# Gated linear attention and a squared-ReLU layer: another opening, joined score stretches, and attention pairs at other places

## The chip, the cores and the metric

The kernel runs on one core of a Trainium2 chip. The time is device microseconds of that core; 523.65 us is the median of three runs of the kernel before (522.74 to 524.44). The engines are named as in the profile: PE (TensorE), DVE (VectorE), ACT (ScalarE), POOL (GpSimd), SP (SyncE, which issues all transfers here).

## What is computed

The inputs q, k, v and alpha have shape (4, 8, 768, 48) in float32. `moe_w_in` (384 x 2048) and `moe_w_out` (2048 x 384) are float64.

```python
for t in range(S):
    state = alpha[:, :, t, :, None] * state + np.einsum('bhd,bhe->bhde', k[:, :, t], v[:, :, t])
    y[:, :, t] = np.einsum('bhd,bhde->bhe', q[:, :, t], state)
...
x = np.ascontiguousarray(attn_out.transpose(0, 2, 1, 3)).reshape(B * S, H * D)
...
h = np.maximum(x @ w_in, 0.0)
return (h * h @ w_out).astype(np.float32)
```

## The kernel before, in words

**Attention blocks.** The 768 steps are cut into 6 chunks of 128, and with 4 batches this makes 24 blocks; block n is chunk n // 4 of batch n % 4. For one block: the logarithm of alpha (`ln`), its running sum by a matmul with a triangle of ones (`cs`), exp of it and of its negative (`eb`, `ei`), q and k scaled by them (`mq`, `mk`), both transposed (`qT`, `kT` in the first four blocks, `turn` for a pair later) and copied from PSUM to SBUF (`qc`, `kc`), products of k and q (`scores`) and of k and v (`state_sums`) in halves of 64 rows, the masked copy of the products (`masked`, called am), the sum with the old state (`sums_copied`, called us) and the next state (`next_state`, called st). The next state is multiplied by the block's last decay: `bl` writes one row of 1.5 KB to DRAM (SP, line 297), `br` reads it back turned into two columns of `last_t` (SP, line 303, two transfers), and DVE multiplies by it on line 421.

**Pairs.** Blocks are worked on in pairs. `ga(a, n)` does scores and state for block n and begins y of the pair a, a+1 that came before; `gb(a, n)` does block n+1 and ends y of the old pair. y is copied into x with `ev` (12 copies per pair, on ACT; for the pairs beginning at 0 and 2, 6 of them on DVE).

**Weights.** Each of the two matrices comes in 8 parts of 768 KB (`load_weights`). The float64 words are turned into float32 in three calls: `convert_first` (2 DVE instructions), `convert_middle` (2 ACT), `convert_second` (3 DVE, lines 175, 179 and 182). Four raw buffers hold parts before conversion. A part of w_in serves two h tiles of 128 columns.

**The dense layers.** The tokens go in 6 groups of 512 (4 blocks). Group 0 runs in plain float32: `ffn_in(0, j)` for 16 h tiles j (3 matmuls each, two records per matmul in the profile, line 805), then the second layer (`layer_out`, `out_plain`, `out_x`, `out_y`, line 701). From group 1 on the products are made in three passes of rounded parts (`in_x`, `in_y`, line 622; `out_x`, `out_y`). For these, x is split (`split_x`, `diff_x`: xa on ACT, xl and xd on DVE), h is split (`split_h`, `diff_h`), and the weights are split once (`prepare`: cast, rest, scale, diff) and kept in DRAM (`keep`), from where `pump` streams them.

**The order.** Nothing is scheduled automatically: each engine runs its instructions in the order in which the program emits them, and each waits for what it needs. The opening is a list of words (`first`), one call per word; it covers blocks 0 to 3, the conversion of the first weight parts, and h tiles 0 and 1, each in two halves of 256 tokens (`ha`, `hb`; the second half needs x of blocks 2 and 3). After that `weave` runs a list of dense units, each with a cost, and emits an event as soon as the costs run reach the event's time. Times for the events are in `AT` and in `PLAN`, in units of these costs: one unit is about 1.3 us. `attention` makes the events of pairs from `PLAN`; `g0`, `g1` and `g` are the places where pairs begin within group 0, group 1 and the later groups, `sc0` stretches them in group 0. Each group has its own call of `weave` with times from 0.

**Transfers.** All transfers are issued by SP in program order. Eight semaphores are used in turn, so a transfer also waits until the one eight places before it has landed.

Of the kernel before, what the change touches and what calls it, by code (L numbers as in the profile page):

```python
# [18 lines left out]
AT = {'evs': 0.4, 'lead': 4, 'post': 3, 'w_first': (46.0, 49.5, 53.0), 'wstep': 1.6, 'w_in_at': 2, 'w_in_by': 3.4, 'room1': 22, 'room': 25, 's0': 4, 'ahead': 6, 'late': 2, 'xs': 0.2, 'g0': (-0.5, 19.5, 28.0), 'sc0': (2.35, 2.35, 2.35), 'g1': (2.5, 19.5, 35.0), 'g': (2.2, 15.0), 'g1x': 50, 'gx': 46, 'g0x': 55.5, 'k0': 2, 'h0': 18, 'k1': 4, 'h1': 4, 'h1by': 2, 'evs0': 0.8, 'tp': 'ADMD', 'tp1': 'ADAD', 'split': 8, 'o0': (40, 47), 'o1': (), 'o2': (23, 26, 29, 35, 42, 36), 'str1': 24, 'ga': 10, 'gb': 12.5}  # L19
# [6 lines left out]
def kernel(  # L26
# [77 lines left out]

    def load(n, xs="aqkv"):
        c, b = divmod(n, B)
        for x in xs:
            t = tile_of(x, n)
            nc.sync.dma_start(  # L109
                out=t[:, :, 0:D] if x in "qk" else t.rearrange("a (h d) -> a h d", h=H),  # L110
                in_=srcs[x][b, :, c * C : (c + 1) * C, :].rearrange("h s d -> s h d"),
            )
# [49 lines left out]
    def convert_middle(i):  # L162
        if moe_w_in.dtype == FP32:
            return
        w, lo, hi, power, upper = half[i]
        nc.scalar.activation(
            out=power, in_=power, func=AF.Relu, scale=2.0**23, bias=rebias
        )
        nc.scalar.activation(out=w, in_=lo, func=AF.Copy, scale=2.0**-52, bias=1.0)

    def convert_second(i):
        if moe_w_in.dtype == FP32:
            return
        w, lo, hi, power, upper = half.pop(i)
# [67 lines left out]
    def ln(n):  # L242
        la = blk[n]["la"] = tile_of("a", n)
        nc.scalar.activation(out=la, in_=la, func=AF.Ln)
# [15 lines left out]
    def cs(n):  # L260

# [26 lines left out]
    def mq(n):  # L288
        scaled("q", n, blk[n]["b"])

    def mk(n):
        scaled("k", n, blk[n].pop("inv"))

    def bl(n):

        if n // B < NCH - 1:
            nc.sync.dma_start(out=rows_t[n], in_=blk[n]["b"][C - 1 : C, :])

    def br(n):
        if n // B < NCH - 1:  # L300
            row = rows_t[n].rearrange("a (p e d) -> (a d) e p", e=2, d=D)
            for e in range(2):
                nc.sync.dma_start(out=last_t[n % 4][64 * e : 64 * e + D, :], in_=row[:, e])  # L303

    def turned(x, n):
        rows = tile_of(x, n).rearrange("a h d -> a (h d)")
# [70 lines left out]
    def masked(n):  # L377
        ps = two[n]
# [10 lines left out]
    def state_sums(n):  # L389
        ps = two[n]  # L390
# [11 lines left out]
    def sums_copied(n):  # L402

        ps = two.pop(n)
# [9 lines left out]
    def next_state(n):  # L414
        blk[n]["s"] = s_t[n % B]
        if n // B < NCH - 1:
            s_all.append(s_t[n % B])
# [12 lines left out]
    def inner(product, m, p, e, h):  # L430
        head = 2 * p + e
        return product(
# [40 lines left out]

    def turn(n):

        for m in (n, n + 1):
            ps = blk[m]["T"] = [bank(m, "T", (2, NP, 64)) for _ in range(2)]
# [14 lines left out]
    def ev_part(n, p):  # L492
        ev(n, (p,))
# [4 lines left out]
    def ev(n, ps=tuple(range(NP))):  # L498
        g, t = divmod(n, GB)
        if t == 0 and ps[0] == 0:  # L500
# [48 lines left out]
    def cast_w(w, p):  # L549
        b = here["b", w, p] = wt("wb", FP32R, shapes[w])  # L550
# [58 lines left out]
    def split_x(g, kk):  # L609
        if kk == 0:  # L610
# [30 lines left out]
    def in_y(j):  # L641
        in_passes(j, "d", "d", False, True)
# [5 lines left out]
    def in_post(j):  # L648
        if kinds[0][j % 4] == "D":
# [31 lines left out]
    def split_h(n, i):  # L681
        r = i % (AHEAD + MORE)
# [34 lines left out]
    def out_plain(p, t, pieces):  # L717
        if p == 0:
# [81 lines left out]
    def ffn_in(g, j, cols=slice(0, GB * C)):  # L800
        w, c0 = w_in[j * NW // NJ], j % (NJ // NW) * 128
        n = cols.stop - cols.start
        ps = ps_ffn.tile([128, GB * C], FP32, tag="att", name="h")[:, 0:n]
        for kk in range(KM):
# [3 lines left out]
            )  # L808
        r = two_k("r")[:, 0:n]
# [10 lines left out]
    def ffn_out(g, t, i):  # L820
# [27 lines left out]
    steps["ha"] = lambda j: ffn_in(0, j, slice(0, HT))  # L848
    steps["hb"] = lambda j: ffn_in(0, j, slice(HT, 2 * HT))
    steps["first"], steps["middle"], steps["second"] = convert_first, convert_middle, convert_second  # L850
    first = """
        ln0 cs0 ei0 mk0 warm0 eb0 bl0 mq0 kT0 load0v kc0 ln1 qT0 load2a load2k cs1
        eb1 qc0 mq1 sc0 bl1 kv0 qT1 load1v ei1 mk1 load2q load3a kT1 ln2 qc1 load3k
        cs2 br0 am0 kc1 eb2 sc1 weights0 br1 us0 kv1 zeros2 bl2 load2v am1 ei2 us1
        load3q ya0 ln3 cs3 yb0 eb3 weights1 mk2 ei3 load3v mq2 qT2 st0 ev0 kT2
        zeros2 zeros2 zeros2 kc2 first0 mk3 middle0 kT3 mq3 br2 load4v qc2 kc3 bl3
        weights2 qT3 sc2 load4q qc3 kv2 second0 am2 br3 first1 sc3 weights3 us2
        load4a kv3 am3 us3 load4k middle1 ha1 second1 ya2 yb2 ev2 weights4 first2
        ha0 hb1 middle2 hb0 st2 st3 st1
    """  # L860
# [28 lines left out]
    def attention(pairs, scale):  # L889


        out = []
        for t, n0, after, *last in pairs:
            for at, fs in EARLY if n0 < SPLIT else PLAN:
                for f in fs.split():
                    w = t + (AT[f] if scale == 1 and f in ("ga", "gb") else at) * scale
                    if f in ("ga", "gb"):
                        given = n0 - 2 if after else None, None if last or n0 >= NBLK else n0
                        out.append((w, {"ga": ga, "gb": gb}[f], given))
                    if f == "gb" and after:  # L900
                        for p in range(NP):
                            out.append((w + AT["evs" if scale == 1 else "evs0"] * p, ev_part, (n0 - 2, p)))
                    if last:
                        continue
                    if f == "ga" and n0 + 3 < NBLK:
                        out.append((w, load, (n0 + 3, "k")))
                    elif f == "gb":
                        for m, x in ((n0 + 2, "v"), (n0 + 3, "v"), (n0 + 4, "k")):
                            if m < NBLK:
                                out.append((w, load, (m, x)))  # L910
                    elif f == "turn":
                        if n0 < NBLK:
                            out.append((w, turn, (n0,)))
                            for m in range(n0 + 2, min(n0 + 4, NBLK)):
                                out.append((w, load, (m, "q")))
                    elif f != "ga" and n0 < NBLK:
                        n = n0 + int(f[-1])
                        out.append((w, steps[f[:-1]], (n,)))
                        if f[:-1] == "cs" and n + 2 < NBLK:
                            out.append((w, load, (n + 2, "a")))  # L920
        return sorted(out, key=lambda x: x[0])

    def weave(units, events):
        at = 0
# [16 lines left out]
    units = [(2, ffn_in, (0, j)) for j in range(2, NJ)]  # L941
    units += layer_out(0) if AT["k0"] else plain_out(0)
    events = [(3.4 * i, next_weights, (3 + i,)) for i in range(2 * NW - 3)]
    events += [(3.4 * i + 1.5, convert_second, (3 + i,)) for i in range(-1, 2 * NW - 3)]
    events += [(0, load, (GB + 1,)), (1.0, load, (GB + 2, "k"))]
    for p, at in enumerate(AT["w_first"]):
        events += prepare(at, "i", p)
    t0, t1, t2 = AT["g0"]
    for pair, scale in zip(((t0, GB, False), (t1, GB + 2, True), (t2, GB + 4, True) + (True,) * (len(AT["g1"]) == 3)), AT["sc0"]):
        events += attention([pair], scale)  # L950
    events += splits_of_x(AT["g0x"], 1)
    order = [*range(NW - AT["k0"], NW), *range(NW - AT["k1"], NW - AT["k0"])]
    order += range(NW - max(AT["k0"], AT["k1"]))
    for p, at in enumerate(AT["o0"]):
        events += prepare(at, "o", order[p])
    weave(units, sorted(events, key=lambda x: x[0]))
    hid.clear()
    acc.clear()
# [14 lines left out]

    for g in range(1, NG):
        events = []
        if g + 1 < NG:
            n = GB * (g + 1) + 2
            *ts, t0, t1 = AT["g1" if g == 1 else "g"]
            pairs = [(t, n - 2, False) for t in ts] + [(t0, n, True), (t1, n + 2, True)]
            events += attention(pairs, 1)  # L980
            events += splits_of_x(AT["g1x" if g == 1 else "gx"], g + 1)
        if g == 1:
            m = len(AT["w_first"])
            for p in range(m, NW):
                events += prepare(AT["w_in_at"] + AT["w_in_by"] * (p - m), "i", p)
            for i, at in enumerate(AT["o1"] + AT["o2"]):
                events += prepare(at, "o", order[len(AT["o0"]) + i])
            n = min(AT["k0"], AT["k1"])
            todo.extend(("l", "o", p) for p in range(NW - n, NW))
            events.append((AT["str1"], stream_out, (AT["k1"], "d")))  # L990
        kinds[0] = AT["tp1" if g == 1 else "tp"]
        room[0] = AT["room1" if g == 1 else "room"]
        events.append((26, stream, (g + 1,)))
# [36 lines left out]
```

## Time and profile before

| what | us |
|---|---|
| median of the runs | 523.65 |
| runs | 522.74, 523.65, 524.44 |
| span of the profiled execution | 520.6 |
| PE busy | 510.8 |
| DVE busy | 366.0 |
| ACT busy | 313.0 |
| POOL busy | 5.4 |

The span is one execution, from the first instruction to the last; the time of a run holds what lies around it too. The granted TensorE clock is 1.000 over the whole span. The page's slices (40 equal ones, busy share in tenths) show where the engines are not full:

```profile
PE   7989999999999999999999999999999999999997
DVE  4798989979978787867597476587465476363861
ACT  4668785677888594575963275963275763164620
DMA  9999687244686787898884788964673534898201
```

One digit is 13 us. Lines of groups give the mean duration of one instruction; "idle before" is the time for which the engine had nothing to do just before instructions of that group, with the instruction that ended it.

### The profile page before, as it was taken

How to read it: one execution, taken by the hardware profiler on the slowest of the kernel's cores; microseconds unless marked ns; L12 is line 12 of the kernel's file. 1: busy time of each engine (PE TensorE's matmuls, PEld its weight loads, DVE VectorE, ACT ScalarE, POOL GpSimd, SP SyncE). 2: the span in 40 equal slices, each digit the busy share in tenths (PEclk: the TensorE clock that was granted, in tenths of full speed). 3: DMA queues.
4: the chain of work that ended last, by engine and by line, in shares of the span. 5: the costliest groups of instructions: out<-in, count | busy, mean ns of one | idle time of the engine just before them, and what ended most of it. 6: DMA issues, size and time to landing. Idle time of an engine off the chain costs nothing.

```text
span 520.6 us, 12925 instructions
## 1 busy us (share of the span) xinstructions
PE 510.8 (98%) x5276; PEld 418.2 (80%) x5276; DVE 366.0 (70%) x631; ACT 313.0 (60%) x650; POOL 5.4 (1%) x29
## 2 busy tenths in 40 slices
PE   7989999999999999999999999999999999999997
PEld 4754455668887668988899988899988899988997
DVE  4798989979978787867597476587465476363861
ACT  4668785677888594575963275963275763164620
POOL 4000000000000000000000000000000000000000
PEclk9999999999999999999999999999999999999999
DMA  9999687244686787898884788964673534898201
GB/s 161 209 278 213 196 240 218 60 114 176 224 200 196 195 246 198 264 317 206 195 248 148 251 246 198 230 187 150 231 255 126 179 126 151 268 340 293 70 0 62
DMA packets 140995, 102.36 MB, mean 197 GB/s; under 512 B 111476, under 2 KB 114568, under 8 KB 140936
## 3 DMA queue, kind: packets, MB, share of 16 engines
q1 hardware_dynamic: 140936, 101.53, 68.3%
q8 instruction: 42, 0.69, 0.6%
q14 instruction: 17, 0.14, 0.1%
HBM read 84.18 MB, written 17.33 MB: 195 GB/s over the span
## 4 chain that ended last, share of the span: by engine, by line
PE 93%; DVE 2%; SPq 2%; DMA 1%; issue 1%; POOL 1%; ACT 0%; POOLq 0%; DVEq 0%
PE o L701 41%; PE h L622 32%; PE h L805 7%; PE y L352 4%; PE T L482 2%; PE sckv L372 2%; PE sckv L395 2%; PE cs L265 1%; DMA qk_lent<-in_q_dram 1%; SPq L303 1%; SPq L109 1%; PE cs L268 1%; PE cs L269 1%; DVE x L515 0%; DVE w_in L182 0%
## 5 line engine op out<-in xcount | busy, mean ns | idle before, releaser
L622 PE MATMUL h<-xa,wb 128*128 128x512 f32 x240 | 68.2, 392 | 0.0
L622 PE MATMUL h<-xl,wl 128*128 128x512 f32 x240 | 67.9, 391 | 0.0
L622 PE MATMUL h<-xd,wd 128*128 128x512 f32 x240 | 67.3, 396 | 0.0
L515 ACT COPY x<-y 32x256 f32<-32x256 f32 (+2 forms) x132 | 47.2, 366 | 25.4 <-PE y L352 20.1
L547 DVE TENSOR_TENSOR hid<-h,hid 128x512 f32<-128x512 f32 x40 | 27.6, 689 | 45.5 <-PE h L622 45.4
L701 PE MATMUL o<-wb,ha 128*128 128x384 f32 x160 | 54.6, 342 | 0.0
L701 PE MATMUL o<-w_out,hid 128*128 128x384 f32 x160 | 54.0, 491 | 0.0
L701 PE MATMUL o<-wd,hd 128*128 128x384 f32 x304 | 53.8, 334 | 0.0
L701 PE MATMUL o<-wl,hl 128*128 128x384 f32 x160 | 53.5, 335 | 0.0
L639 ACT ACTIVATE h<-h 128x512 f32<-128x512 f32 x40 | 23.3, 582 | 49.7 <-PE h L622 49.7
L622 PEld LDWEIGHTS h<-xl,wl 128*128 128x128 f32 x240 | 45.1, 188 | 10.0 <-DVE xl L547 0.4
L701 PEld LDWEIGHTS o<-wd,hd 128*128 128x128 f32 x304 | 52.7, 188 | 0.3 <-DVE osb L737 0.3
L622 PEld LDWEIGHTS h<-xa,wb 128*128 128x128 f32 x240 | 44.6, 188 | 9.3 <-ACT xa L596 0.2
L622 PEld LDWEIGHTS h<-xd,wd 128*128 128x128 f32 x240 | 44.2, 188 | 9.2
L701 PE MATMUL o<-wb,hx 128*128 128x384 f32 x144 | 48.7, 338 | 0.0
L701 PE MATMUL o<-wl,hx 128*128 128x384 f32 x144 | 48.1, 334 | 0.0
L701 PEld LDWEIGHTS o<-w_out,hid 128*128 128x128 f32 x160 | 29.8, 190 | 19.3
L637 ACT ACTIVATE hid<-h 128x512 f32<-128x512 f32 x40 | 24.0, 600 | 34.6 <-PE h L622 34.5
L805 PE MATMUL h<-x,w_in 128*128 128x512 f32 (+1 forms) x108 | 43.6, 552 | 1.2 <-ACT x L515 1.2
L596 ACT ACTIVATE ha<-hid 128x512 fp32r<-128x512 f32 x40 | 25.6, 639 | 25.5 <-DVE hx L547 16.1
L805 PEld LDWEIGHTS h<-x,w_in 128*128 128x128 f32 x108 | 19.9, 190 | 21.1 <-issue 17.2
L547 DVE TENSOR_TENSOR hl<-hid,ha 128x512 fp32r<-128x512 f32 x40 | 27.5, 688 | 10.1 <-ACT ha L596 10.1
(114 smaller groups left out, 879.7 us busy)
## 6 DMA issues: line engine op xcount, KB each, us to landing
wd<-do SPq DMA_DIRECT2D x36, 384.0 KB, 3.7
wl<-lo SPq DMA_DIRECT2D x34, 384.0 KB, 4.0
wl<-li SPq DMA_DIRECT2D x32, 384.0 KB, 3.5
wd<-di SPq DMA_DIRECT2D x32, 384.0 KB, 3.9
raw<-in_moe_w_in_dram SPq DMA_DIRECT2D x8, 768.0 KB, 5.6
raw<-in_moe_w_out_dram SPq DMA_DIRECT2D x8, 768.0 KB, 5.6
v_in<-in_v_dram SPq DMA_DIRECT2D x24, 192.0 KB, 4.7
out_dram<-osb SPq DMA_DIRECT2D x24, 192.0 KB, 1.9
```

The costliest lines, as they stand in the source:

```text
L352: ins = nc.tensor.matmul(out=ys[e][64 * half : 64 * half + D + G * e, m % 2, p // 2, t], lhsT=lhsT, rhs=rhs, start=(half, e) not in seen, ...
L372: nc.tensor.matmul(out=ps[e][HALF[h], 0, p, :], lhsT=ks[rows, p, HALF[h]], rhs=qs[rows, p, HALF[h]], start=True, stop=True, skip_group_che ...
L395: nc.tensor.matmul(out=ps[h][64 * e : 64 * (e + 1), 1, p, G:64], lhsT=tile_of("k", n)[HALF[h], 2 * p + e, :], rhs=tiles["v"][n % NV][HALF[ ...
L482: nc.tensor.transpose(out=ps[h][:, i, p, :], in_=rows[HALF[h], 128 * p : 128 * (p + 1)], identity=ident[HALF[h], HALF[h]],)
L515: copy(out=x[kk][to : to + m, t : t + 2], in_=blk[n]["y"][e][r : r + m, :, p // 2],)
L547: nc.vector.tensor_tensor(out=o, in0=x, in1=z, op=op)
L596: nc.scalar.activation(out=a, in_=x, func=AF.Copy, scale=NEAR)
L622: nc.tensor.matmul(out=acc["h", j], lhsT=here[w, "i", p][:, kk, jj * 128 : (jj + 1) * 128], rhs=x_parts[x][:, kk], start=start and kk == 0 ...
L637: nc.scalar.activation(out=hid[j], in_=x, func=AF.Copy, scale=E)
L639: nc.scalar.activation(out=x, in_=x, func=AF.Copy, scale=1.0 + E)
L701: nc.tensor.matmul(out=acc[t][:, 0:DM], lhsT=lhs[:, t * C : (t + 1) * C], rhs=rhs, start=start, stop=stop, skip_group_check=True,)
L805: nc.tensor.matmul(out=ps, lhsT=w[:, kk, c0 : c0 + 128], rhs=xT[g][kk][:, cols], start=(kk == 0), stop=(kk == KM - 1),)
```

## The change

The list `first` becomes an entry of `AT` and has another order. Weight part 0 is loaded after a of block 2 and converted between the steps of blocks 0 to 3; seven parts instead of five are loaded within the list. Four h tiles (0 to 3) run in it, in halves of 256 tokens, instead of two. The writing back of block 0's last row (`bl0`) and its reading (`br0`) stand later in it. The filler matmuls are fewer: `zeros2` appears two times in place of four, `warm0` stays once.

The new function `joined` does scores, state and y of a pair in one stretch in place of `ga` and `gb`; `attention` uses it where an entry has a place for it (`whole_at`): the pair of blocks 4, 5 and the pair 8, 9, neither with an older pair's y. All groups now share one call of `weave`, so an event may cross from one group into the next; the times of a group are counted from its own beginning (`base`). The dense part of group 0 begins with the tiles that the opening left (`halves`), at the cost count where it would have been (`begin`, here 4). The times in `AT` differ almost throughout. The `need` and `given` calls check the order while the program is built and emit no instruction.

```diff
-AT = {'evs': 0.4, 'lead': 4, 'post': 3, 'w_first': (46.0, 49.5, 53.0), 'wstep': 1.6, 'w_in_at': 2, 'w_in_by': 3.4, 'room1': 22, 'room': 25, 's0': 4, 'ahead': 6, 'late': 2, 'xs': 0.2, 'g0': (-0.5, 19.5, 28.0), 'sc0': (2.35, 2.35, 2.35), 'g1': (2.5, 19.5, 35.0), 'g': (2.2, 15.0), 'g1x': 50, 'gx': 46, 'g0x': 55.5, 'k0': 2, 'h0': 18, 'k1': 4, 'h1': 4, 'h1by': 2, 'evs0': 0.8, 'tp': 'ADMD', 'tp1': 'ADAD', 'split': 8, 'o0': (40, 47), 'o1': (), 'o2': (23, 26, 29, 35, 42, 36), 'str1': 24, 'ga': 10, 'gb': 12.5}
+AT = {'evs': 0.65, 'lead': 4, 'post': 3, 'w_first': (45.25, 42.0, 51.5), 'wstep': 1.6, 'w_in_at': 2.5, 'w_in_by': 3.4, 'room1': 22, 'room': 25, 's0': 4, 'ahead': 6, 'late': 2, 'xs': 0.2, 'g0': ((1.5, 4, False, True, 28.25), (20.25, 6, True, True), (28.75, 8, True, False)), 'sc0': (2.35, 2.35, 2.35), 'g1': ((5.5, 8, False, 15.5), (15.5, 10, True), (34.5, 12, True)), 'g': ((1.7, 6, True), (15.5, 8, True)), 'g1x': 50.0, 'gx': 48.25, 'g0x': 55.25, 'k0': 2, 'h0': 16, 'k1': 4, 'h1': 3, 'h1by': 2, 'evs0': 0.3, 'tp': 'ADMD', 'tp1': 'ADAD', 'split': 8, 'o0': (44.75, 47.25), 'o1': (), 'o2': (21.75, 27.5, 31.75, 35.0, 41.25, 41.75), 'str1': 22.0, 'ga': 9.5, 'gb': 13.0, 'cv0': 1.5, 'first': 'ln0 warm0 cs0 load0v ei0 mk0 kT0 eb0 mq0 qT0 ln1 kc0 qc0 cs1 load2a eb1 ei1 sc0 mq1 weights0 ln2 mk1 kv0 load1v am0 qT1 us0 bl1 qc1 kT1 first0 kc1 sc1 load2k middle0 load2q kv1 am1 load3a cs2 load3v load2v weights2 br1 ei2 us1 ya0 eb2 yb0 zeros2 ln3 zeros2 mk2 load3k mq2 kT2 ev0 qT2 kc2 bl0 cs3 second0 qc2 eb3 first1 sc2 load3q kv2 ei3 mk3 load4q bl2 mq3 middle1 ha0 qT3 qc3 kT3 am2 kc3 weights6 second1 ha1 sc3 us2 load4k weights1 br2 br0 kv3 st0 bl3 ha2 am3 us3 load4v first2 ya2 weights3 br3 yb2 st3 ev2 middle2 ha3 hb3 second2 weights5 st2 hb0 weights4 load4a hb1 st1 hb2'}
...
+    def joined(a, n):
+
+        if n is None:
+            ga(a, None)
+            gb(a, None)
+            return
+        product = y_begin(a) if a is not None else None
+
+        def sums(m):
+            for f in (scores, state_sums, masked, sums_copied):
+                f(m)
+
+        sums(n)
...
+        next_state(n)
+        sums(n + 1)
...
+        next_state(n + 1)
...
-    steps["ha"] = lambda j: ffn_in(0, j, slice(0, HT))
-    steps["hb"] = lambda j: ffn_in(0, j, slice(HT, 2 * HT))
+    def half_in(x, j):
+        given.add(("h" + x, j))
+        ffn_in(0, j, slice(0, HT) if x == "a" else slice(HT, 2 * HT))
+
+    steps["ha"] = lambda j: half_in("a", j)
+    steps["hb"] = lambda j: half_in("b", j)
...
-    first = """
-        ln0 cs0 ei0 mk0 warm0 eb0 bl0 mq0 kT0 load0v kc0 ln1 qT0 load2a load2k cs1
-        eb1 qc0 mq1 sc0 bl1 kv0 qT1 load1v ei1 mk1 load2q load3a kT1 ln2 qc1 load3k
-        cs2 br0 am0 kc1 eb2 sc1 weights0 br1 us0 kv1 zeros2 bl2 load2v am1 ei2 us1
-        load3q ya0 ln3 cs3 yb0 eb3 weights1 mk2 ei3 load3v mq2 qT2 st0 ev0 kT2
-        zeros2 zeros2 zeros2 kc2 first0 mk3 middle0 kT3 mq3 br2 load4v qc2 kc3 bl3
-        weights2 qT3 sc2 load4q qc3 kv2 second0 am2 br3 first1 sc3 weights3 us2
-        load4a kv3 am3 us3 load4k middle1 ha1 second1 ya2 yb2 ev2 weights4 first2
-        ha0 hb1 middle2 hb0 st2 st3 st1
-    """
+    first = AT["first"]
...
+                if f in ("ga", "gb") and whole_at is not None:
+                    w = whole_at
...
+                if f == "ga":
+                    out.append((w, ga if whole_at is None else joined, given))
...
-    units = [(2, ffn_in, (0, j)) for j in range(2, NJ)]
...
-    events = [(3.4 * i, next_weights, (3 + i,)) for i in range(2 * NW - 3)]
-    events += [(3.4 * i + 1.5, convert_second, (3 + i,)) for i in range(-1, 2 * NW - 3)]
...
+    halves = {j: {x for x in "ab" if ("h" + x, j) in given} for j in range(NJ)}
+    units = []
...
+    units += [(2, ffn_in, (0, j)) for j in range(NJ) if not halves[j]]
+    begin = 2 * NJ - 4 - sum(u[0] for u in units)
...
+    events = [(3.4 * i + cv0, next_weights, (3 + i,)) for i in range(-3, 2 * NW - 3) if ("mid", 3 + i) not in given]
+    events += [(3.4 * i + cv0 + 1.5, convert_second, (3 + i,)) for i in range(-3, 2 * NW - 3) if ("w", 3 + i) not in given]
...
-        weave(layer_in(g) + layer_out(g), events)
...
+    weave(units, sorted(events, key=lambda x: x[0]), begin)
```

## The prediction

> **What bounds the kernel now.** I read the page's busy table first, then its chain by engine.
>
> ```profile
> PE 510.8 (98%) x5276; PEld 418.2 (80%) x5276; DVE 366.0 (70%) x631; ACT 313.0 (60%) x650; POOL 5.4 (1%) x29
> ...
> PE 93%; DVE 2%; SPq 2%; DMA 1%; issue 1%; POOL 1%; ACT 0%; POOLq 0%; DVEq 0%
> ```
>
> TensorE (PE) sets the end, but "98%" hides one place. The windows before and after 35.29 us show it (columns: window, its length, then busy time of PE, PEld, DVE, ACT, POOL, then granted clock, DMA share, GB/s):
>
> ```profile
> 0.00:35.29 35.29, 30.00 (x536) 21.97 (x537) 24.50 (x50) 18.36 (x38) 5.36 (x29) 1.00 1.03 204
> 35.29:517.20 481.91, 480.78 (x4740) 396.19 (x4740) 341.00 (x582) 294.63 (x613) 0.00 (x0) 1.00 0.67 197
> ```
>
> After 35.29 TensorE idles 1.1 us of 482: only less matmul work can help there, and only a new wait can hurt. Before 35.29 it runs fillers (warm, zeros) and waits. DMA share there is 1.03 (transfers overlap), so the opening is held by transfers. The chain in order of time (start, length) says what ends it:
>
> ```profile
> 18.25 5.06 DMA qk_lent<-in_q_dram
> ...
> 34.42 0.43 DVE x L515
> 34.87 0.37 ACT x L515
> 35.29 9.72 PE h L805 x26
> 45.01 0.65 PE cs L265 x2
> 45.66 2.57 PE h L805 x6
> ```
>
> q of block 3 lands at 23.31 us, VectorE (DVE) works without a pause, the copies of y of blocks 2 and 3 into x end at 35.24, and dense work begins. One full h tile is six records, 2.57 us. So the tile j=4, the fifth, starts at 45.01 - 2.57 = 42.44 us. It is my mark, since the change leaves exactly the tiles from j=4 on to the dense part.
>
> **The change part by part.** *Two more h tiles in the opening.* Dense work loses 2 x 2.57 = 5.14 us. After the last copy before, TensorE still ran 8 records of 256 columns (0.215 us each: zeros x18 took 4.05 us with its drain) and j=2 began 2.05 us after 35.24. After the change 20 such records follow: 20 x 0.215 + 0.33 = 4.63 us. At equal copies the mark would come 42.44 - (35.24 + 4.63) = 2.57 us sooner. The gain hangs on when the copies end.
>
> *Transfers in the opening.* The queue on SyncE (SP) takes them in program order. Two places of the SP timeline give the prices; the windows beneath give the rates:
>
> ```profile
> 18.87 2.58 SPq L126 DMA_DIRECT2D raw<-in_moe_w_in_dram  x1
> ...
> 21.50 0.49 SPq L109 DMA_DIRECT2D v_in<-in_v_dram  x1
> ```
>
> ```profile
> 10.00:15.00 5.00, 4.65 (x110) 3.65 (x111) 2.28 (x8) 2.36 (x5) 0.00 (x0) 1.00 1.36 190
> 15.00:17.40 2.40, 1.93 (x69) 1.44 (x68) 1.45 (x5) 0.52 (x1) 0.00 (x0) 1.00 0.59 71
> 18.00:20.00 2.00, 2.00 (x43) 1.79 (x43) 1.30 (x4) 1.54 (x4) 0.00 (x0) 1.00 1.07 344
> ```
>
> A block of 192 KB moves at 190 GB/s: 1.0 us. A weight part of 768 KB at 344 GB/s: 2.3 us. v of block 3 was issued at 21.50 behind the second part and landed only at 26.69 (sckv of L395 waits for it): a transfer stands behind those issued earlier. Landing lags the data by some 0.9 us. The 71 GB/s stretch is a hole: the queue ran dry. Up to q of block 3 the sum without holes is 2.2 (first data) + 15 blocks + 2.35 = 19.5 us, but its data ended near 22: 2.4 us of holes.
>
> The changed kernel's SP order is: first six blocks, v0, a2, w part 0, v1, row 1, k2, q2, a3, v3, v2, part 1, last 1, k3, row 0, q3, q4, row 2, part 2, k4, part 3, last 2, last 0. Row and last are the two legs by which a block's decay reaches `last_t` (br, L303), wanted by next_state (L421). The pair "last 0", ahead of both first weight parts before, is now the last of this list: its first data waits for 18 blocks and four parts: 2.2 + 18.0 + 4 x 2.35 + 0.4 (the small ones) + 0.9 = 30.9 us without holes. With before's 2.4 us of holes it is 33.3; I take that, because the new list has as many changes between block and weight transfers. Its range is 30.9 to 35.7 (twice the holes).
>
> *Who waits for it.* In the changed DVE order, multiplying block 0's state by `last` (L421) stands ahead of am3, us3 and the x copies. Without the wait DVE would reach it thus: q3 lands at 2.2 + 16 + 4.7 + 0.3 + 0.9 = 24.1 (26.5 with holes); then mq3 0.47, am2 0.67, the second part's last three conversion steps 2.73, us2 and s 0.73: 28.7 to 31.1 us. So it waits about 2.2 us. Behind it are queued am3 (0.66), us3, the second half of y on TensorE, and the copies. From rows of before: L421 0.36, am 0.66, us3's start to the end of y 2.1 (29.07 to 31.15), copies 2.67, last ACT copy 0.4: 6.2 us. Copies end at 33.3 + 6.2 = 39.5, the mark at 39.5 + 4.63 = 44.1: 1.7 us later than 42.44 (the two tiles' gain is inside this difference). Ends: 30.9 gives -0.7, 35.7 gives +4.1.
>
> *Conversion moved earlier.* Its DVE and ACT steps lie under the transfers, so they cost nothing while q3 is late; second2 (3 steps, 2.73 us) and middle2 (1.8) lie under the 4.63 us of h records.
>
> *End of the first layer.* The last pair's second y stretch (gb) moves behind one more out_x group; 16 + 16 records of o now follow it, not 40. Rows of ACT and TensorE there:
>
> ```profile
> 120.41 1.15 ACT L515 COPY x<-y 32x256 f32<-32x256 f32 x3 [1.02 <-PE y L352]
> ...
> 122.94 3.32 ACT L515 COPY x<-y 64x256 f32<-64x256 f32 x9
> 126.28 1.68 ACT L596 ACTIVATE xa<-x 128x512 fp32r<-128x512 f32 x3
> ```
>
> ```profile
> 124.69 3.07 PE L701 MATMUL o<-wd,hd 128*128 128x384 f32 x16
> 127.60 0.91 PE L622 MATMUL h<-xa,wb 128*128 128x512 f32 x3
> ```
>
> TensorE now reaches L622 32 x 0.175 + 0.2 = 5.8 us after y. ACT needs 4.4 (copies) + 0.74 (one wl, where two jobs stood) + three xa at 0.52 to 0.64, so xa ends at 6.9, and xl of DVE at 7.8 instead of the 7.2 that L622 would want. Counting the wait on each pass, 1.0 us of stall where 0.3 lay before: +0.7 (0 to 1.2).
>
> *Two pairs of scores in one stretch* (blocks 4, 5 and 8, 9): the first scores after a matmul of 128 rows take 0.62 us, those after y 0.46, and the first h pass afterwards 0.13 more. Two stretches fewer: 2 x 0.29 = -0.6. The later load of k7 (DVE has some 10 us in hand: w_out part 0 is ready at 70.3, used at 79.8) and the pairs placed elsewhere cost nothing while DVE and ACT keep that cover; uncovered, each would cost up to 1 us, kept for the range.
>
> **Sum:** 520.6 + 1.7 + 0.7 - 0.6 = 522.4 us of span. Around the span lie 523.65 - 520.6 = 3.05 us, so 525.4 us.
>
> **Rivals.** *A: the rows come in time* (faster). If "last 0" overtakes or DVE is never held, q3 alone sets the opening: 24.1 to 26.5, + 4.6 + 6.2 + 4.63, so the mark at 39.5 to 41.9; the middle, 40.7, is 1.7 early: 520.6 - 1.7 + 0.1 + 3.05 = 522.0 us. For: the row needs a few KB only. Against: v3's 5.2 us. The Trainium skill (DMA: Bandwidth & Descriptors, "Queues, rings and completion order") says that each DMA engine consumes a ring's descriptors in order; by that no overtaking is left, only fewer holes, and the trace's v3 agrees.
>
> *B: the array slows* (slower still). While DVE waits, TensorE has nothing from us2's products, near 31 us, to us3, near 34.5; the fillers in that gap are gone. Before, no gap after the start exceeds 1.1 us. In the first microseconds a record of 256 columns took 2.93/6 = 0.49 us, not 0.215. If a gap of 3 us brings that pace back for some eight records, they cost 8 x 0.27 = 2.2 us: 527.6 us. It decides once the gap nears 3 us. The Trainium skill (TensorE: Matmul & The Clock Gate, "Part 1: The HAM clock gate") lets an idle window of about 3.4 us halve the clock; no gap in this trace is long enough to show it.
>
> *C: weight parts late.* With TensorE two tiles ahead, part 3 is ready about 0.8 us before use, and mq5 about 1 us before its transposes; before, part 3 had 48.88 - 44.83 = 4 us. Both missing by 1 us: 527.4 us. Against: every DVE step in that count is at its measured length.
>
> *D: nothing moves.* Fewer holes (1.0 us, last 0 at 31.9) bring the mark to +0.3: 524.0 us. It is the forecast's lower side.
>
> **How the numbers follow.** 0.3% is 1.6 us, about what a measurement of this kernel can tell from no change. The forecast with D has 0.47; its own range is 523.0 to 527.8, and 0.24 of it lies within 0.3%, 0.23 above. A has 0.25 (0.21 faster, 0.04 within), B 0.18 and C 0.10 (slower). Faster 0.21, same 0.28, slower 0.51. The range runs from A's 522.0 less half a microsecond to B's 527.6 plus half of one.
>
> **What would show it.** The wait of DVE's L421 on "last" near 31 to 33 us; no such wait would sink the forecast. The mark near 44 us. PE idle of about 0.7 us more where L622 begins. Cold records of h or y in the opening speak for B, waits of L805 on DVE for C. A mark before 41 us makes it wrong.

## The result, and the profile after

The changed kernel takes 528.32 us (median of 4 runs, 527.43 to 528.67) beside 523.19 us for the kernel before on the same chip: ratio 1.0089, 95% interval 1.0071 to 1.0106. It is slower by 5 us, in the forecast's direction but past its range (525.4; 521.5 to 528.1). The profiled execution has a span of 525.7 us, 5.1 more than before. Line numbers from here on are those of the changed kernel; L421 before is L457 now, L805 is L896, L622 is L703, L701 is L786.

The busy table and the chain by engine of the changed kernel, from its page:

```profile
PE 510.9 (97%) x5276; PEld 421.6 (80%) x5276; DVE 363.8 (69%) x631; ACT 313.7 (60%) x654; POOL 5.3 (1%) x29
...
PE 76%; DVE 9%; ACT 7%; DMA 4%; issue 2%; SPq 2%; DVEq 0%; POOLq 0%
```

TensorE is busy for as long as before (510.9 against 510.8 us) and idle for 5 us more (14.8 against 9.8). Busy time holds fillers and slow records too, so the table does not say where the time goes. The chain in order of time does (start, length, what):

```profile
23.77 2.94 DMA row<-b
...
29.45 5.25 DMA last<-row
...
34.82 0.36 DVE s L457
35.18 0.68 DVE am L410 x2
35.86 0.26 DVE us L440
...
36.16 1.59 PE y L379 x47
...
37.85 1.13 PE y L379 x31
38.98 8.52 PE h L896 x30
```

Before, q of block 3 and VectorE's own work stood in this place; now it is the second leg of row 0, 5.25 us from its issue to its landing. Two entries of VectorE's timeline (start, length, in brackets the idle time before and what ended it):

```profile
34.82 0.36 DVE L457 TENSOR_TENSOR s<-s,last 128x192 f32<-128x192 f32 x1 [4.22 <-DMA last<-row]
...
38.58 0.36 DVE L457 TENSOR_TENSOR s<-s,last 128x192 f32<-128x192 f32 x1 [1.26 <-DMA last<-row]
39.04 2.67 DVE L594 COPY x<-y 32x256 f32<-32x256 f32 x6
```

The first wait is the forecast's, 4.2 us long instead of 2.2. The second is for row 3 (block 3's new state, `st3`, stands ahead of the x copies); it ends as y ends, so here it costs nothing of its own (in the second profile of this kernel, after_again below, it held the copies up by some 0.5 us). In windows (length, busy time of PE, PEld, DVE, ACT, POOL, then granted clock, DMA share, GB/s):

```profile
31.00:35.00 4.00, 1.15 (x20) 0.65 (x18) 0.18 (x1) 0.80 (x2) 0.00 (x0) 1.00 0.89 186
35.00:36.00 1.00, 0.00 (x0) 0.00 (x0) 1.00 (x4) 0.00 (x0) 0.00 (x0) 0.91 1.02 399
36.00:38.00 2.00, 1.71 (x54) 1.52 (x58) 1.31 (x4) 0.00 (x0) 0.00 (x0) 0.50 0.89 246
38.00:40.00 2.00, 2.00 (x35) 1.70 (x35) 1.26 (x4) 0.50 (x2) 0.00 (x0) 0.50 0.68 254
40.00:42.00 2.00, 2.00 (x6) 1.61 (x5) 1.63 (x4) 1.59 (x5) 0.00 (x0) 0.50 0.01 3
```

TensorE has nothing from 32.14 to 36.16 us, and then runs at half clock until some 42.6 us. That costs time in two places. From the start of L457 to the start of the copies it took 4.22 us, where the variants below with a late row and a full clock (ha3_fill, fill2_st3) took 3.15. From the start of the copies to the mark it took 8.28 us, where five other profiles took 7.55 (after_again and swap_st3 among them, whose clock fell too but was back by 41.1 us). So the half clock cost 1.07 + 0.73 = 1.8 us here.

The mark (start of tile j=4) is two tiles of 2.58 us ahead of the cs that begins at 52.47 in TensorE's timeline: 47.3 us. The forecast's 42.44 took the start of cs from the chain (45.01); TensorE's timeline has it at 44.85 before, so in one and the same reading the mark before is 42.3, and the changed kernel's is 5.0 us later. Behind it 478.4 us are left, 478.3 before. So 5.0 of the 5.1 us come from the opening.

### The profile page after: what moved, and what is told of

Same layout as the page of the kernel before. It is cut to its first block, busy times and chain, and to the rows that moved or that the text cites. A ratio compares the mean times of both kernels' runs of the same rounds, so it can differ in the third digit from the quotient of the medians.

```text
span 525.7 us, 12899 instructions
## 1 busy us (share of the span) xinstructions
PE 510.9 (97%) x5276; PEld 421.6 (80%) x5276; DVE 363.8 (69%) x631; ACT 313.7 (60%) x654; POOL 5.3 (1%) x29
## 4 chain that ended last, share of the span: by engine, by line
PE 76%; DVE 9%; ACT 7%; DMA 4%; issue 2%; SPq 2%; DVEq 0%; POOLq 0%
PE h L703 32%; PE o L786 32%; PE y L379 4%; ACT power L177 2%; PE T L556 2%; PE h L896 2%; PE sckv L399 2%; PE sckv L427 1%; SPq L119 1%; DVE w_out L192 1%; DVE w_out L195 1%; DMA wd<-do 1%; DMA v_in<-in_v_dram 1%; DVE wl L626 1%; DMA last<-row 1%
## 5 line engine op out<-in xcount | busy, mean ns | idle before, releaser
L703 PE MATMUL h<-xa,wb 128*128 128x512 f32 x240 | 68.8, 395 | 0.0
L703 PE MATMUL h<-xl,wl 128*128 128x512 f32 x240 | 67.8, 391 | 0.0
L703 PE MATMUL h<-xd,wd 128*128 128x512 f32 x240 | 66.6, 392 | 0.0
L594 ACT COPY x<-y 32x256 f32<-32x256 f32 (+2 forms) x132 | 47.3, 365 | 23.1 <-PE y L379 12.8
L626 DVE TENSOR_TENSOR hid<-h,hid 128x512 f32<-128x512 f32 x40 | 27.5, 688 | 41.5 <-PE h L703 38.8
L786 PE MATMUL o<-wd,hd 128*128 128x384 f32 x304 | 54.4, 335 | 1.4 <-DVE osb L823 1.0
L786 PEld LDWEIGHTS o<-wd,hd 128*128 128x128 f32 x304 | 52.7, 188 | 2.4 <-DVE osb L823 1.4
L786 PE MATMUL o<-wb,ha 128*128 128x384 f32 x160 | 54.1, 338 | 0.0
L786 PE MATMUL o<-w_out,hid 128*128 128x384 f32 x160 | 53.5, 490 | 0.0
L786 PE MATMUL o<-wl,hl 128*128 128x384 f32 x160 | 53.5, 334 | 0.0
L703 PEld LDWEIGHTS h<-xl,wl 128*128 128x128 f32 x240 | 45.0, 188 | 10.0 <-DVE xl L626 0.3
L703 PEld LDWEIGHTS h<-xd,wd 128*128 128x128 f32 x240 | 44.6, 188 | 9.1
L703 PEld LDWEIGHTS h<-xa,wb 128*128 128x128 f32 x240 | 44.3, 188 | 9.2
L786 PE MATMUL o<-wb,hx 128*128 128x384 f32 x144 | 48.7, 338 | 0.0
L786 PE MATMUL o<-wl,hx 128*128 128x384 f32 x144 | 48.1, 334 | 0.0
L786 PEld LDWEIGHTS o<-w_out,hid 128*128 128x128 f32 x160 | 29.9, 190 | 19.7
L896 PE MATMUL h<-x,w_in 128*128 128x512 f32 (+1 forms) x120 | 44.8, 528 | 0.1
L896 PEld LDWEIGHTS h<-x,w_in 128*128 128x128 f32 x120 | 23.7, 201 | 17.7 <-issue 14.4
```

What stands on the lines that cost most here:

```text
L594: copy(out=x[kk][to : to + m, t : t + 2], in_=blk[n]["y"][e][r : r + m, :, p // 2],)
L626: nc.vector.tensor_tensor(out=o, in0=x, in1=z, op=op)
L703: nc.tensor.matmul(out=acc["h", j], lhsT=here[w, "i", p][:, kk, jj * 128 : (jj + 1) * 128], rhs=x_parts[x][:, kk], start=start and kk == 0 ...
L786: nc.tensor.matmul(out=acc[t][:, 0:DM], lhsT=lhs[:, t * C : (t + 1) * C], rhs=rhs, start=start, stop=stop, skip_group_check=True,)
L896: nc.tensor.matmul(out=ps, lhsT=w[:, kk, c0 : c0 + 128], rhs=xT[g][kk][:, cols], start=(kk == 0), stop=(kk == KM - 1),)
```

## The experiments

Ratios are to the kernel before on the same chip, with 95% intervals. "Mark" is read from TensorE's timeline in each run's one profile; in this reading the kernel before has 42.3. What is left behind the mark ranges from 478.1 to 481.3 us in these profiles, and only part of that is explained below, so mark and median need not move together.

| run | median, us | ratio | mark, us |
|---|---|---|---|
| changed kernel | 528.32 | 1.0089 (1.0071 to 1.0106) | 47.3 |
| changed kernel again (after_again) | 527.33 | 1.0090 (1.0077 to 1.0103) | 47.0 |
| row0_early | 527.54 | 1.0082 (1.0066 to 1.0098) | 46.9 |
| row0_st3 | 523.69 | 1.0016 (1.0004 to 1.0028) | 42.4 |
| row0_mid | 522.89 | 1.0009 (0.9999 to 1.0019) | 41.6 |
| swap_st3 | 527.86 | 1.0094 (1.0076 to 1.0111) | 46.5 |
| before_row0_late | 530.57 | 1.0146 (1.0131 to 1.0162) | 50.3 |
| ha3_st3 | 528.15 | 1.0090 (1.0076 to 1.0103) | 45.9 |
| ha3_fill | 527.29 | 1.0096 (1.0082 to 1.0111) | 44.9 |
| fill2_st3 | 529.06 | 1.0117 (1.0098 to 1.0136) | 46.2 |
| fill_st3 | 540.61 | 1.0335 (1.0310 to 1.0361) | 53.6 |
| old_opening | 523.66 | 1.0008 (0.9999 to 1.0018) | 42.6 |
| joined_off | 527.54 | 1.0080 (1.0063 to 1.0097) | 47.1 |
| mid_end40 | 523.98 | 1.0019 (1.0006 to 1.0031) | 44.4 |
| mid_end48 | 525.30 | 1.0043 (1.0031 to 1.0055) | 43.8 |
| row0_st3_fill12 | 523.03 | 1.0005 (0.9994 to 1.0016) | 42.4 |
| best1 | 526.44 | 1.0066 (1.0048 to 1.0085) | 45.9 |
| best2 | 523.32 | 1.0029 (1.0005 to 1.0053) | 42.3 |

### Is it the rows?

row0_early, edits in the word list:

```diff
-... us0 bl1 qc1 ... weights2 br1 ei2 ... kc2 bl0 cs3 ... weights1 br2 br0 kv3
+... us0 bl0 bl1 qc1 ... weights2 br0 br1 ei2 ... kc2 cs3 ... weights1 br2 kv3
```

> The changed kernel with both legs of row 0 issued beside those of row 1 (before w_in parts 2 and 3), nothing else changed. Theory 1 (the forecast's mechanism, sized anew: row 0 lands at 34.8 us behind the weight parts, VectorE waits 4.2 us in L457, TensorE idles 4.0 us and then runs at half clock): the first L457 no longer waits and the first half of y starts near 31.5 instead of 36.2 us; but the second L457, on row 3, still stands ahead of the x copies and its transfer still goes behind part 3, so copies start no earlier than row 3 lands, 36 to 38.5 us: 526 to 528 us, a gain of 0.3 to 2. Theory 2 (row 0 alone holds the opening): the whole 4.9 us come back, 523 to 523.5 us. Theory 3 (weight parts and block 3 hold it, rows only seem to): under 0.5 us of gain and another wait in the place of L457.

row0_st3, the same and:

```diff
-... yb2 st3 ev2 middle2
+... yb2 ev2 st3 middle2
```

> As the one with row 0 early, and the new state of block 3 (which reads row 3) is computed behind the x copies instead of ahead of them. Theory 1: no row is waited for ahead of the copies. VectorE reaches block 0's multiplication at 30.6 us as before, and 6.2 us later the copies end, 36.8; with TensorE at full clock the mark (start of h tile j=4) is at 36.8 + 4.6 = 41.4 us, 5.9 earlier than in the changed kernel: 522.4 us, about 0.8 under the kernel before. Theory 2 (only row 0 matters): same as the one with row 0 alone early, within 0.4 us. Theory 3 (transfers of block 3 and weights hold it): 527 or more.

row0_early gained less than 1 us, row0_st3 some 4 us, which leaves it 0.16% above the kernel before: theory 1 in both by the direction and the order of the waits. In row0_st3 the time is 1.3 us above theory 1's 522.4, and the mark 1.0 us behind its 41.4: VectorE reached L457 without any wait, but at 31.55 and not at 30.6 us. VectorE in row0_early:

```profile
31.16 0.36 DVE L457 TENSOR_TENSOR s<-s,last 128x192 f32<-128x192 f32 x1
...
37.41 0.36 DVE L457 TENSOR_TENSOR s<-s,last 128x192 f32<-128x192 f32 x1 [3.77 <-DMA last<-row]
37.80 2.67 DVE L594 COPY x<-y 32x256 f32<-32x256 f32 x6
```

The first wait is gone and the second, hidden before, takes its place: 3.77 us for row 3, still ahead of the copies, which begin only 1.2 us sooner. With that multiplication behind the copies (row0_st3) they begin at 34.88 and the mark is at 42.4. Two waits stood in line; taking away the first alone shows nearly nothing. Nor does the second word alone: swap_st3 below has block 3's state behind the copies and row 0 late, and its ratio is the changed kernel's (1.0094).

before_row0_late puts the wait into the kernel before:

```diff
-... cs2 br0 am0 ... qT2 st0 ev0 ... load4a kv3 am3 us3
+... cs2 am0 ... qT2 ev0 ... load4a br0 kv3 st0 am3 us3
```

> The kernel before, with only row 0's second leg (the read into last) moved behind the fourth weight part's and the last blocks' loads, and the multiplication that reads it moved to just ahead of block 3's masking, as the changed kernel has it. Theory 1 (a late row alone makes the loss): VectorE gets there near 28.3 us and waits until the row lands, 32 to 35 us; the gap of TensorE exceeds 3 us and y runs at half clock: 527.5 to 531 us, so slower than before by 4 to 8. Theory 2 (a small transfer is not held by the weight parts, and the loss of the changed kernel has to do with its fewer fillers and its dense part): within 1 us of the kernel before, 523.2.

7.8 us slower than before, theory 1. VectorE's line there (L421 is the multiplication):

```profile
35.80 0.36 DVE L421 TENSOR_TENSOR s<-s,last 128x192 f32<-128x192 f32 x1 [7.32 <-DMA last<-row]
```

The gap on TensorE was 8.3 us and its clock 0.50 from some 32.4 to 42.6 us. So the place of one read of 1.5 KB, together with that of the multiplication that needs it, is enough for a loss of this size, with the old dense part and the old fillers.

### Why 34.8 us and not 33.3?

swap_st3: row 0's second leg ahead of row 2's, still behind both weight parts.

```diff
-... weights1 br2 br0 kv3 ... yb2 st3 ev2
+... weights1 br0 br2 kv3 ... yb2 ev2 st3
```

> The changed kernel with the second legs of rows 2 and 0 in the other order (row 0's first), still behind w_in parts 2 and 3, and block 3's new state behind the x copies. In the changed kernel SyncE held row 0's second leg behind row 2's, which had to wait until row 2's first leg had landed (26.7 us). Theory 1 (that hold is why row 0 landed at 34.8 us and not at the 33.3 of the forecast): it lands near 33.3, TensorE's gap falls to about 2.5 us, the clock stays at 1.00, and the mark comes near 44.1 us, so 525.0 to 525.6. Theory 2 (the bytes of the two parts ahead of it set the landing): 34.4 us or later, a gap of 3.5 us or more, 527.8 or more.

row0_mid: row 0's second leg ahead of part 3 (`weights1` loads w_in part 3).

```diff
-... load4k weights1 br2 br0 kv3 ... yb2 st3 ev2
+... load4k br0 weights1 br2 kv3 ... yb2 ev2 st3
```

> The changed kernel with row 0's second leg moved ahead of w_in part 3 alone (part 2 and the blocks stay ahead of it), row 2's left behind part 3, and block 3's new state behind the x copies. Theory 1 (the bytes ahead of row 0 set its landing): one part of 768 KB less, 2.2 to 2.4 us, so it lands at 32.4 to 32.6 instead of 34.8 us; VectorE waits about 2 us instead of 4.2, TensorE's gap is below 2 us, the clock stays at 1.00 and the mark comes 4 us sooner, near 43.3: 524.0 to 524.8 us. Theory 2 (all that is issued then lands together at 34 to 35 us): no change, 528.

> The changed kernel itself once more, beside the two below on the same chip, as their measure: 528.0 to 528.6 us by every theory.

VectorE's multiplication in swap_st3, and then in row0_mid:

```profile
34.74 0.36 DVE L457 TENSOR_TENSOR s<-s,last 128x192 f32<-128x192 f32 x1 [4.04 <-DMA last<-row]
```

```profile
30.79 0.36 DVE L457 TENSOR_TENSOR s<-s,last 128x192 f32<-128x192 f32 x1 [0.32 <-DMA last<-row]
34.11 2.67 DVE L594 COPY x<-y 32x256 f32<-32x256 f32 x6 [1.09 <-PE y L379]
```

The swap moved nothing (34.74 against 34.82), so the hold on SP was not it. With part 3 behind it the row landed 34.74 - 30.79 = 3.95 us sooner in row0_mid, and the time is 4.4 us under the changed kernel measured beside it (522.89 against 527.33, itself under the 528.0 to 528.6 expected of it). swap_st3 has block 3's state late as well, so one word that moved past one other, `br0` past `weights1`, makes the difference between these two.

The 3.95 us are more than theory 1's 2.2 to 2.4, but they are no price of a part. mid_end48 below has row0_mid's opening, and there the row landed at 33.14. Counted from the issue of part 2, the row took 9.9 to 10.7 us behind two parts (swap_st3 24.86 to 34.74, changed kernel 24.20 to 34.82) and 6.9 to 8.0 behind one (row0_mid 23.93 to 30.79, mid_end48 25.17 to 33.14): some 1.9 to 3.9 us for a part, about 3, where the forecast had 2.35. The bytes did not move slowly: in the changed kernel the rate was 269 to 361 GB/s in each microsecond from 27 to 32 us, then 178 and 101, and the row came 0.8 us later. What fills these last microseconds is not shown. The Trainium skill (DMA: Bandwidth & Descriptors, "Queues, rings and completion order") has each DMA engine take its descriptors in order; both runs agree.

### What does the half clock cost?

fill_st3, the fillers 17 and 14, and fill2_st3 with 8 and 6:

```diff
-        for _ in range(3):
+        for _ in range({2: 3, 0: 17, 1: 14}[n]):
...
-... first2 ya2 ... yb2 st3 ev2 middle2 ha3 hb3
+... first2 zeros0 ya2 ... yb2 ev2 st3 middle2 ha3 zeros1 hb3
```

> The changed kernel with row 0 as late as it has it, but 17 filler matmuls ahead of y of blocks 2 and 3, where TensorE waits for row 0, and 14 more while the x copies run; block 3's new state goes behind the x copies. VectorE's wait of 4.2 us stays. Theory 1 (the gap drops the granted clock, which costs 1.1 us in y and 0.6 us in h): the clock stays at 1.00, y ends 1.3 us sooner, copies start with it, the mark comes 1.7 to 1.9 us sooner: 526.4 to 526.7 us. Theory 2 (the clock drops for another reason, or its cost is hidden under the transfers): 527.8 to 528.5, slow records as before. Theory 3 (fillers get in the way): slower than 528.5.

> The run with fillers again, with 8 and 6 of them instead of 17 and 14, since one filler matmul took 0.44 us there (two records), not 0.22. Row 0 stays late and VectorE's wait of about 4.1 us stays. Theory 1 (the gap drops the granted clock, and that costs time of its own): the clock is 1.00 from 20 us on, y of blocks 2 and 3 takes 1.5 us behind the wait instead of 2.4, the x copies start 1.3 us sooner than in the changed kernel, and h runs at full pace behind them: 1.9 us in all, 526.4 us. Theory 2 (the clock costs nothing because the rows and parts set the end): 527.8 to 528.5.

fill_st3 misjudged the filler (0.44 us each, not 0.22): its 31 fillers took 13.7 us and delayed y by 3 us, so its time says nothing. With 8 and 6 the clock was 1.00 and y of am took 1.49 instead of 2.37 us, theory 1 by the records. But the median, 529.06, lies above what either theory allows. The fillers behind y also held up h, which began at 41.07 us, some 0.8 us after the last copy, so this run does not settle what the clock costs.

ha3_st3 puts useful work into the gap, and ha3_fill also five fillers behind y:

```diff
-... bl3 ha2 am3 ... yb2 st3 ev2 middle2 ha3 hb3
+... bl3 ha2 ha3 am3 ... yb2 ev2 st3 middle2 [zeros1] hb3
```

> The changed kernel with one half tile of h (1.46 us of TensorE's work, no filler) moved ahead of y of blocks 2 and 3, into the gap, and block 3's new state behind the x copies. Row 0 stays late, VectorE's wait of about 4 us stays. Theory 1 (a gap of 2.5 us leaves the clock at 1.00, one of 4.0 does not): y takes 1.5 us behind the wait instead of 2.4, and the mark comes 1.0 to 1.9 us sooner: 526.4 to 527.4 us. Theory 2 (the clock falls all the same, or the copies and not the array set the mark): 528 or more.

> As the run with a half tile of h moved into the gap, and five fillers (0.44 us each) behind y of blocks 2 and 3, where that run's clock fell to 0.50 at 39.2 us because TensorE then waited for the x copies. Row 0 stays late. Theory 1 (the half clock costs time of its own): the clock is 1.00 from 20 us on, and the mark is near 45.5 us, 1.8 sooner than in the changed kernel beside it: its median less 1.3 to 1.9 us. Theory 2 (it costs nothing, since the copies set the mark): within 0.6 us of the changed kernel beside it.

ha3_st3 kept y at full pace: VectorE waited only 1.93 us in this execution, since it came to the row late, and TensorE's gap was 0.43 us. But while the copies ran TensorE idled again and the clock fell at 38.8 us. Its time, 528.15, is theory 2's. ha3_fill, TensorE from the gap on:

```profile
35.53 0.46 PE L379 MATMUL y<-qs,us 48*48 48x64 f32 x16 [2.26 <-DVE us L440]
35.80 1.49 PE L379 MATMUL y<-am,v_in 64*48 64x64 f32 x64
37.21 2.42 PE L365 MATMUL zeros<-s 128*128 128x256 f32 x10
39.48 10.72 PE L896 MATMUL h<-x,w_in 128*128 128x256 f32 x36
```

A gap of 2.26 us, the clock at 1.00 in every window from 12 us on, and the mark 2.1 us sooner than in the changed kernel beside it (44.9 against 47.0): theory 1 as far as the mark. But the median is the same (527.29 against 527.33). The two traces show where the gain went. Starts of the same scores and cs matmuls lie 2.0 us apart until 172 us, 1.0 from 180 us on and 0.6 from 228 us on. ha3_fill has two stalls there that the changed kernel has not (the brackets: idle time, "issue" where it waited for nothing that the profile shows):

```profile
174.56 3.81 PE L786 MATMUL o<-w_out,hid 128*128 128x384 f32 x11 [0.71 <-issue]
...
206.61 0.34 PE L786 MATMUL o<-wl,hx 128*128 128x384 f32 x1 [0.60 <-issue]
```

The kernel before has one of the kind (0.96 us at 204 us), fill2_st3 two of 1.4 us together. Nor is all of the 2.1 us at the mark the clock's: 0.5 is the row, which landed at 34.19 instead of 34.69, and another 0.5 the wait for row 3 ahead of after_again's copies. That leaves some 1.1 us for the clock there and, with the 0.73 above, 1.8 in the changed kernel's first profile. That it costs as much at the end is not shown, since both runs that kept the clock up had such stalls later.

### The dense part

old_opening: the changed kernel with the word list of the kernel before.

> The changed kernel's dense part (joined stretches, new places of the pairs) behind the opening list of the kernel before, with two h tiles in the opening. Theory 1 (the opening makes the whole loss, the dense part nearly nothing, as the forecast had it with +0.1): 522.7 to 523.6 us. Theory 2 (the dense part costs of its own): 525 or more. Theory 3 (it saves): under 522.

523.66 us, ratio 1.0008: theory 1; the dense part as a whole costs nothing that can be measured, and the opening makes the loss.

joined_off takes the joined stretches apart:

```diff
-'g0': ((1.5, 4, False, True, 28.25), ... 'g1': ((5.5, 8, False, 15.5),
+'g0': ((1.5, 4, False, True), ... 'g1': ((5.5, 8, False),
```

> The changed kernel with the two joined stretches of scores (blocks 4, 5 and 8, 9) taken apart again, nothing else. The forecast put the joining at -0.6 us (two fewer changes between matmuls of 64 and of 128 rows, 0.29 each). Theory 1: 528.9 us. Theory 2 (joining saves nothing, since the second half moves a wait): 528.2 to 528.4. Theory 3 (it costs, by longer stretches that VectorE has to follow): under 528.

Inconclusive: its interval covers the changed kernel's, and its profile (span 526.4, mark 0.2 sooner) has 0.9 us more behind the mark.

mid_end40 and mid_end48 are row0_mid with the last pair of the first group elsewhere, for the term "end of the first layer" (28.0 in mid_end40, 27.25 in mid_end48):

```diff
-'g0': ( ... (28.75, 8, True, False))
+'g0': ( ... (28.0, 8, True, False))
```

> The kernel with row 0's second leg ahead of w_in part 3 and block 3's state late, and in the dense part the last pair of the first group placed so that 40 records of o follow its last y again, as in the kernel before, instead of 32. The forecast put the changed end of the first layer at +0.7 us (0 to 1.2). Theory 1 (that term is real): from the mark to the first matmul of the second layer 85.2 to 85.8 us instead of 86.5, and 0.7 to 1.2 us off the median: 521.7 to 522.2, just under the kernel before. Theory 2 (the wait at the layer's end only moves): 522.7 to 523.1, no change.

> As the one with 40 records of o behind the last y, with 48. Theory 1: no wait is left there, so 0 to 0.3 us under the one with 40, 521.5 to 522.2. Theory 2: no change against the one with 32, 522.7 to 523.1, or slower, where the pair's earlier place holds something else.

No gain: theory 2, which for mid_end48 allows the loss that it has. (Their marks lie later than row0_mid's, with the same opening: in these two profiled executions w_in part 0 was taken up at 15.5 and 14.7 us instead of 13.3.) From the mark to the first matmul of the second group (L703) it is 85.3 us before, 86.1 in the changed kernel, 86.5 in row0_mid, 86.7 and 87.8 in these two. The stall is not at L703 but one step ahead, in the changed kernel:

```profile
130.46 3.07 PE L786 MATMUL o<-wd,hd 128*128 128x384 f32 x16 [1.03 <-DVE osb L823]
```

In mid_end40 the same wait is 1.38 us long, in mid_end48 1.44. VectorE adds up o (osb) behind the splitting of h and of weights. Before, it came there at 124.09 us, while TensorE's sums still ran (the last began at 124.39); in the changed kernel it comes at 129.86, behind the last at 129.09. An earlier place of y did not remove the wait.

### Towards a faster version

row0_st3_fill12 adds three fillers at 12 to 15 us to row0_st3; best1 and best2 also move k and q of block 3 ahead of part 1 and the conversion of part 1 behind block 3's sums, best1 the conversion of part 0 ahead of the copies of blocks 0 and 1 as well. The edit of the first:

```diff
-... kc1 sc1 load2k middle0 load2q kv1
+... kc1 zeros1 sc1 load2k middle0 load2q zeros3 kv1
```

> The kernel with row 0 early and block 3's new state behind the x copies, and besides three fillers in TensorE's two holes between 12 and 15 us. All variants of the changed kernel so far show the clock at 0.50 from 15.5 to 18.5 us too, where the kernel before has 1.00. Theory 1 (a second, earlier half-clock stretch, made by holes of under 1 us each): the clock stays at 1.00, y of blocks 0 and 1 ends up to 1.5 us sooner; but q of block 3 lands near 27 us all the same and VectorE then waits for that, so the time falls by 0 to 0.6: 523.1 to 523.7. Theory 2 (the early stretch is on the path all the way): the whole 1.5 us, 522.2. Theory 3 (holes so short don't lower the clock, and fillers change nothing): the clock drops again.

> The run with fillers at 12 to 15 us, and four more words moved: k and q of block 3 loaded ahead of w_in part 1 and of v of block 3, the three DVE steps that finish w_in part 0 ahead of the copies of y of blocks 0 and 1, those that finish part 1 behind block 3's sums, the h half tile of part 1 behind y of blocks 2 and 3. Theory 1 (with the rows out of the way VectorE's queue ahead of block 3's sums, and q of block 3, set the opening): block 3's sums come near 27 us, the copies end near 33 to 34 and the mark is at 39 to 40.5 us: 520.3 to 521.8, under the kernel before. Theory 2 (TensorE or the weight parts set it by then): no more than 0.5 under the run with row 0 early and block 3's state late: 523.2 or more.

> A second attempt at a faster opening: row 0 early, block 3's state late, fillers at 12 to 15 us, k and q of block 3 loaded ahead of w_in part 1, the second half tile of h (part 0) while q of block 3 is awaited, part 1's last three steps behind block 3's sums, its h half tile behind y. Unlike the first attempt, ScalarE's copies of block 2's turned q and k and its exponentials keep their places, and part 0's last steps stay behind the copies of blocks 0 and 1. Theory 1 (VectorE's queue ahead of block 3's sums sets the opening): sums of block 3 near 29.5 us, copies end near 35.5, mark 41.0 to 41.5, 1.0 to 1.4 sooner than with row 0 early alone: 521.6 to 522.1 us. Theory 2 (TensorE's own work sets it): 522.5 to 523.2, no better than the kernel before.

row0_st3_fill12 kept the clock up and the mark where it was, theory 1. best1 lost: VectorE's copies of blocks 0 and 1 began only at 19.9 us behind the conversion, ScalarE's wait for those, and block 2's turned q stands behind them on ScalarE; TensorE idled 1.8 us for it and its clock fell twice. best2 brought block 3's sums to 30.0 us and the copies' begin to 33.1, but the mark only to 42.3: theory 2 by the time, though what holds the mark there is not shown. No version is measurably faster than the kernel before; row0_mid and row0_st3_fill12 equal it.

## Why the prediction was right in kind and wrong in size

- *What bounds the kernel, and the mark.* Held: the dense part costs 478.4 us behind the mark, 478.3 before.
- *Who waits for row 0.* Held: L457 on `last`, TensorE idle from us2's products to us3, VectorE there at 30.6 us (forecast 28.7 to 31.1). row0_mid beside swap_st3, and before_row0_late, show it as the cause. The forecast did not have block 3's new state, which waits for row 3 between L457 and the copies: the changed kernel hides it behind y, row0_early does not.
- *Full clock behind the gap.* This step failed. The sum put the half clock at nothing and left it to rival B, as if B took the forecast's place; but both hang on the same wait. The forecast's own gap, 31 to 34.5 us, is 3.5 us long and met B's condition, "once the gap nears 3 us". Measured: a gap of 4.0 us, the clock at 0.50 behind it, and 1.8 us more to the mark (1.07 in y, 0.73 in h). B's own price, 2.2 us, was near. It belonged into the forecast, and on top of the latest landing too: 4.1 + 1.8 for the mark, which would have held the measured 5.0.
- *"last 0" lands at 33.3 us.* This term was too small. It landed at 34.8, within its own bounds (30.9 to 35.7) but 1.5 us late, and the 1.5 us pass one to one to the mark. A part ahead of the row cost about 3 us where the forecast had 2.35, but the bytes moved at the usual rate, so which term of the landing's sum was short stays open. Forecast 1.7, row 1.5 and clock 1.8 make the 5.0 us.
- *A (the rows come in time).* Not what happened, and where the variants made the rows come in time the gain was not there either: marks at 41.6 and 42.4 instead of 40.7, and 522.89 us, ratio 1.0009, in the best. Overtaking, its mechanism, is not seen: in swap_st3 and the changed kernel the row came behind both parts.
- *Conversion moved earlier: nothing.* Held for the rows' late state. With the rows in time no mark is below 41.6 us, so at most 0.7 of the two tiles' 2.57 us was seen; what holds the rest is open.
- *End of the first layer: +0.7.* The size fits, 86.05 - 85.33 = 0.7 us, but by luck: it comes at another place, L786 waiting for VectorE's osb, which the forecast had among what VectorE's cover hides.
- *Joined stretches: -0.6.* Behind the first matmul of the second group the profile has 0.75 us less, but before's issue stall of 1.0 us lies there too; joined_off leaves it open.
- *C (weight parts late).* Not seen: no wait of L896 on VectorE in the dense part.

## What to carry to other kernels

A small transfer costs what stands ahead of it in its queue, so look who needs it; and price the large ones by how much later something behind them landed, not by the rate of their bytes alone. Where a wait opens a gap on TensorE, add the slower clock behind it to the same case, and look for the next wait in line before expecting the gain of taking the first away. A gain in an opening is compared at a mark, since small stalls later on can hide or feign a microsecond.

## What the runs showed of the hardware

The clock fell without any long gap, too. In the traces of this case all changes of the clock lie at whole multiples of 3.41 us from the first one, at another phase in each execution, so windows are cut at these steps here. The changed kernel, and swap_st3 in the same stretch of the program:

```profile
11.93:15.34 3.41, 1.80 (x66) 1.41 (x66) 1.51 (x4) 2.14 (x4) 0.00 (x0) 1.00 1.29 245
15.34:18.76 3.42, 3.29 (x86) 2.35 (x88) 1.83 (x5) 1.48 (x4) 0.00 (x0) 0.50 0.95 144
```

```profile
13.71:17.12 3.41, 2.08 (x67) 1.45 (x71) 2.05 (x5) 2.19 (x4) 0.00 (x0) 1.00 0.97 166
17.12:20.53 3.41, 3.28 (x87) 2.87 (x77) 2.89 (x7) 2.02 (x7) 0.00 (x0) 1.00 0.91 196
```

In the changed kernel no gap from 12 to 15 us exceeds 0.86 us, TensorE is busy for 1.80 of the step's 3.41 us, and the next step has half the clock. With 2.08 of 3.41 us swap_st3 kept it. From 8 to 60 us of these traces the clock fell after steps with up to 0.55 of busy time (ha3_st3 1.87 us of 3.41, longest gap 1.30) and stayed after those with 0.60 and more (ha3_fill 2.06). That is a pattern of these runs, with few exceptions outside the stretch, and no proof of a threshold. The early fall cost nothing that shows: in row0_st3_fill12 and after_again, where the clock stayed up, VectorE then waited for q of block 3 (0.52 and 0.35 us), which came no sooner.

The Trainium skill (TensorE: Matmul & The Clock Gate, "Part 1: The HAM clock gate") tells of an idle window of about 3.4 us, running freely. The step of 3.41 us agrees, and so do the gaps of 4.0 us, which held a whole idle step from 32.41 to 35.82 us (half clock), and of 2.3 us (full). Where the step was only half idle, the measurement decides: that was enough here.
